# Attention's two narrow matmuls, split into halves of 64 weight columns, in a kernel of linear attention and a low-rank mixer

## The chip, the cores and the metric

The kernel runs on one core of one Trainium2 chip. The metric is the device time of one execution in microseconds. Engines are named as in the profile: PE is TensorE, and PEld is its weight loads, which run beside the matmuls; DVE is VectorE, ACT ScalarE, POOL GpSimd, SP SyncE. A line number such as L487 is a line of the kernel.

## What is computed

Eight images (`b`) with eight heads of 576 tokens and 64 features each go through linear attention, and its output through a token mixer and a two-layer network:

```python
def phi(x):                                    # 128 features, then twice 128
    proj = einsum('bhsd,df->bhsf', x, w_phi)
    proj = proj - max(abs(proj), axis=-1)
    return concatenate([exp(proj), exp(-proj)], axis=-1)
q_p, k_p = phi(q), phi(k)
kv  = einsum('bhsf,bhsd->bhfd', k_p, v)        # 256 x 64 a head
z   = sum(k_p, axis=2)
num = einsum('bhsf,bhfd->bhsd', q_p, kv)
den = einsum('bhsf,bhf->bhs', q_p, z) + 1e-06
x   = num / den                                # 576 x 512 an image
u   = x + (x.T @ U @ V).T
out = u + relu(u @ w_ch1) @ w_ch2              # 512 -> 2048 -> 512
```

## The kernel before

Heads go in pairs (class `Pair`): 32 pairs, four to an image. Of 576 tokens 512 are treated as four tiles of 128 (`NT = 4`), and the 64 left over ("tail") in matmuls of their own. `v` lies beside a column of ones, so that one matmul with 65 moving columns (`D + 1`) gives kv and z together, and another gives num and den together.

- `kv_main` (L445 to L450) makes kv of one head. For each token tile `t` and each half `f` of the 256 features, the weights are 128 features of `kp` (128 tokens by 128 columns) and the moving data is `vb`, 65 columns. The result is added up over `t` in `kv_ps`, in PSUM. That is 8 matmuls a head, behind the tail's two (`kv_tail`, L441, with both heads' 130 columns). `kv_done` then copies it out on DVE (L454).
- `out_main` (L482 to L489) makes num and den. For each of four blocks `c` of 128 tokens, two matmuls over `f` take 128 tokens of `qp` as weights and 65 columns of `kv` as moving data. That is 8 matmuls a call and two calls a pair, behind the tail's two (`out_tail`, L474). `normalize` then divides on DVE (L461 to L466).

Both work in plain float32. Such a matmul of the program appears in the profile as two weight loads and two matmuls, so 512 matmuls of the program on each of the lines L448 and L487 are 1024 records there.

The network of an image (class `Mixer`) has matmuls with 512 moving columns: `hidden` (L631) and `add` (L652), 16 blocks each. They are queued as chunks in `todo`, and `Pace` hands them out between the steps of the next image's attention, so that TensorE works on image b's network while the other engines prepare the attention of image b + 1. The last stretch of the program, from 1018 us on, holds network work alone. Before the first network is ready, matmuls on zeros (`keep_busy`, L758) are put between the steps. Within these bounds a scheduler that estimates durations sets the order of each engine's instructions.

One more matmul plays a part below: `Tokens.up` (L585) takes 128 columns of `v_all` as weights, but for the tail of every second image only 64.

Of the kernel before, what the change touches and what calls it, by code (L numbers as in the profile page):

```python
# [21 lines left out]
P = 128  # L22
# [3 lines left out]
def tile_kernel(  # L26
# [12 lines left out]
    nc = tc.nc  # L39
    B, H, S, D = q.shape  # L40
    F = w_phi.shape[1]
# [6 lines left out]
    NT = S // P  # L48
# [200 lines left out]
            nc.vector.tensor_sub(dst_lo, src, f32(dst_hi)))  # L249


    SPLIT, Q = 2, 32

    class Pair:

# [189 lines left out]
        def kv_main(self, g, kp):  # L445
            for t in range(NT):
                for f in range(2):
                    nc.tensor.matmul(  # L448
                        self.kv_v[:, f, g, :], kp[:, t, f * F:(f + 1) * F], self.vb[:, g, t, :],
                        start=False, stop=(t == NT - 1), skip_group_check=True)  # L450

        def kv_done(self):
            self.kv = small.tile([P, 2, 2, D + 1], F32, tag="kv", bufs=1, name=f"kv{self.nm}")
# [28 lines left out]
        def out_main(self, s, qp, x):  # L482
            xp = self.ps(f"xp{s}_", True)
            xv = xp[:, 0:NT * (D + 1)].rearrange("p (c e) -> p c e", e=D + 1)
            for c in range(NT):
                for f in range(2):
                    nc.tensor.matmul(  # L487
                        xv[:, c, :], qp[:, f, c * P:(c + 1) * P],
                        self.kv[:, f, c // 2 if self.split else s, :],  # L489
                        start=(f == 0), stop=(f == 1))  # L490
            if not self.split:
                h = self.h0 + s
                self.normalize(s, xv, x[:, :, h * D:(h + 1) * D])
                return
            xo = x.rearrange("p (s z) c -> p s z c", s=2)[:, s, :, self.h0 * D:(self.h0 + 2) * D]
            self.normalize(s, xv, xo.rearrange("p z (g d) -> p g z d", g=2))
# [452 lines left out]
```

## Time and profile before

| | |
|---|---|
| time, median of 2 runs | 1218.99 us (1218.80 to 1219.19) |
| the profiled execution, its own time | 1219.22 us |
| its span in the profile | 1217.4 us |
| PE busy, PEld busy | 1193.5 us (98%), 1029.9 us (85%) |
| DVE, ACT, POOL busy | 667.5, 537.2, 204.9 us (55%, 44%, 17%) |
| granted TensorE clock, mean over the span | 0.995 |

About 1.8 us of the profiled execution lie outside the span. Busy times of PE and PEld count an instruction from its issue to its modelled end, and neighbours overlap; how far apart neighbours start tells more than how long one lasts. A timeline row merges neighbours of one kind: its start, its length to the last one's end, and their number after the x.

### The profile page before, as it was taken

How to read it: one execution, taken by the hardware profiler on the slowest of the kernel's cores; microseconds unless marked ns; L12 is line 12 of the kernel's file. 1: busy time of each engine (PE TensorE's matmuls, PEld its weight loads, DVE VectorE, ACT ScalarE, POOL GpSimd, SP SyncE). 2: the span in 40 equal slices, each digit the busy share in tenths (PEclk: the TensorE clock that was granted, in tenths of full speed). 3: DMA queues.
4: the chain of work that ended last, by engine and by line, in shares of the span. 5: the costliest groups of instructions: out<-in, count | busy, mean ns of one | idle time of the engine just before them, and what ended most of it. 6: DMA issues, size and time to landing. Idle time of an engine off the chain costs nothing.

```text
span 1217.4 us, 18242 instructions
## 1 busy us (share of the span) xinstructions
PE 1193.5 (98%) x6669; PEld 1029.9 (85%) x6669; DVE 667.5 (55%) x1482; ACT 537.2 (44%) x1151; POOL 204.9 (17%) x154
## 2 busy tenths in 40 slices
PE   6999998999999999999999999999999999999998
PEld 5977887888888888888888888888888888888886
DVE  5667678765566556764647556765656542311211
ACT  5778787454443545344435454344444431111110
POOL 3334444211110111011111111011101110000000
PEclk8999999999999999999999999999999999999999
DMA  4686121331235123431244123521343015410201
GB/s 115 218 273 238 48 62 30 104 99 30 65 95 111 42 48 87 87 99 30 66 121 108 29 54 85 130 49 29 93 102 99 1 53 145 119 35 1 69 1 35
DMA packets 248290, 100.61 MB, mean 83 GB/s; under 512 B 215304, under 2 KB 227848, under 8 KB 248200
## 3 DMA queue, kind: packets, MB, share of 16 engines
q1 hardware_dynamic: 246928, 98.16, 30.9%
q10 hardware_dynamic: 1272, 1.28, 0.4%
q8 instruction: 53, 0.87, 0.3%
q14 instruction: 37, 0.30, 0.1%
HBM read 78.41 MB, written 20.97 MB: 82 GB/s over the span
## 4 chain that ended last, share of the span: by engine, by line
PE 88%; DVE 5%; DMA 2%; ACT 2%; SPq 1%; issue 1%; POOL 0%; DVEq 0%; ACTq 0%; POOLq 0%
PE ph L631 31%; PE o L652 30%; PE kv_ps L448 8%; PE xp L487 8%; PE pk L404 2%; PE pp L567 1%; PE kv_ps L441 1%; PE xpt L474 1%; PE pq L427 1%; PE pq L428 1%; SPq L270 1%; PE pq L432 1%; DVE w L240 1%; PE vp L585 1%; PE pk L389 1%
## 5 line engine op out<-in xcount | busy, mean ns | idle before, releaser
L631 PE MATMUL ph<-uT_hi,w 128*128 128x512 f32 x1152 | 389.3, 395 | 1.7 <-ACT uT_hi L248 1.1
L652 PE MATMUL o<-w,h_hi 128*128 128x512 f32 x1152 | 327.7, 395 | 0.7 <-ACT h_hi L636 0.7
L631 PEld LDWEIGHTS ph<-uT_hi,w 128*128 128x128 f32 x1152 | 216.3, 188 | 46.8 <-ACT uT_hi L248 1.8
L652 PEld LDWEIGHTS o<-w,h_hi 128*128 128x128 f32 x1152 | 211.1, 188 | 41.9 <-ACT h_hi L636 1.4
L631 PE MATMUL ph<-uT_lo,w 128*128 128x512 f32 x576 | 225.0, 391 | 0.3 <-DVE uT_lo L249 0.3
L636 ACT ACTIVATE h_hi<-ph 128x512 fp32r<-128x512 f32 x144 | 86.0, 597 | 278.9 <-PE ph L631 268.0
L637 DVE SCALAR_TENSOR_TENSOR h_lo<-ph,h_hi 128x512 fp32r<-128x512 f32 x144 | 98.7, 685 | 176.7 <-ACT h_hi L636 175.4
L652 PE MATMUL o<-w,h_lo 128*128 128x512 f32 x576 | 192.2, 395 | 0.0
L368 POOL PARTITION_ALL_REDUCE qp<-qp x64 | 127.0, 1984 | 296.8 <-ACT qp L367 274.8
L487 PEld LDWEIGHTS xp<-kv,qp 128*128 128x128 f32 x1024 | 122.6, 192 | 5.4 <-ACT w L239 0.8
L448 PEld LDWEIGHTS kv_ps<-vb,kp 128*128 128x128 f32 x1024 | 124.3, 192 | 2.8
L631 PEld LDWEIGHTS ph<-uT_lo,w 128*128 128x128 f32 x576 | 108.3, 188 | 21.6 <-DVE uT_lo L249 0.8
L487 PE MATMUL xp<-kv,qp 128*128 128x65 f32 x1024 | 122.9, 272 | 1.1 <-DVE x L466 0.7
L448 PE MATMUL kv_ps<-vb,kp 128*128 128x65 f32 x1024 | 123.7, 270 | 0.0
L652 PEld LDWEIGHTS o<-w,h_lo 128*128 128x128 f32 x576 | 105.2, 188 | 20.5 <-DVE h_lo L637 0.2
L358 ACT ACTIVATE kp<-kp 128x512 f32<-128x512 f32 x64 | 40.4, 632 | 125.9 <-DVE kp L355 88.7
L368 POOL PARTITION_ALL_REDUCE qp_t<-qp_t x32 | 27.3, 853 | 401.1 <-ACT qp_t L367 401.1
L324 DVE TENSOR_TENSOR T<-raw,T 64x512 fp32r<-64x512 f32 x96 | 68.2, 711 | 34.0 <-ACT T L323 31.5
L323 ACT CAST T<-raw 64x512 fp32r<-64x512 f32 x96 | 59.4, 618 | 34.7 <-PE pq L428 26.0
L320 DVE STREAM_TRANSPOSE raw<-raw 128x512 f32<-128x512 f32 x48 | 34.1, 711 | 67.8 <-DMA raw<-in_q_dram 24.8
L370 ACT ACTIVATE qp<-qp 128x512 f32<-128x512 f32 x64 | 40.4, 632 | 50.6 <-DVE qp L369 50.1
L145 POOL INT64_ADD w_ab<-w_ab x32 | 44.9, 1404 | 67.8 <-DVE w_ab L141 63.0
(125 smaller groups left out, 1324.2 us busy)
## 6 DMA issues: line engine op xcount, KB each, us to landing
words<-in_moe_w_ch_dram SPq DMA_DIRECT2D x32, 512.0 KB, 8.4
w<-kept SPq DMA_DIRECT2D x30, 512.0 KB, 4.0
vb<-in_v_dram SPq DMA_DIRECT2D x64, 128.0 KB, 2.4
u_dram<-x SPq DMA_DIRECT2D x32, 256.0 KB, 2.1
st<-u_dram SPq DMA_DIRECT2D x16, 512.0 KB, 3.8
out_dram<-st SPq DMA_DIRECT2D x32, 256.0 KB, 2.3
y<-u_dram SPq DMA_DIRECT2D x112, 64.0 KB, 2.2
raw<-in_k_dram SPq DMA_DIRECT2D x192, 32.0 KB, 1.8
```

What stands on the lines that cost most here:

```text
L145: nc.gpsimd.int64_add(a64, a64, b64)
L323: nc.scalar.copy(out=m[here, s, :], in_=x_[here])
L324: nc.vector.tensor_sub(m[there, s, :], x_[here], f32(m[here, s, :]))
L358: nc.scalar.activation(out=kp[:, :, 0:F], in_=kp[:, :, F:2 * F], func=AF.Exp)
L368: nc.gpsimd.partition_all_reduce(qp[:, 0, :], qp[:, 1, :], P, ReduceOp.absmax)
L370: nc.scalar.activation(out=qp[:, 0, :], in_=qp[:, 1, :], func=AF.Exp)
L448: nc.tensor.matmul(self.kv_v[:, f, g, :], kp[:, t, f * F:(f + 1) * F], self.vb[:, g, t, :], start=False, stop=(t == NT - 1), skip_group_ch ...
L487: nc.tensor.matmul(xv[:, c, :], qp[:, f, c * P:(c + 1) * P], self.kv[:, f, c // 2 if self.split else s, :], start=(f == 0), stop=(f == 1))
L631: nc.tensor.matmul(ph, w1_part(f, l, c), r[:, c, :], start=(n == 0), stop=(n == 3 * NCC - 1))
L636: on_act = nc.scalar.activation(out=h_hi, in_=ph, func=AF.Relu)
L637: on_dve = nc.vector.scalar_tensor_tensor(out=h_lo, in0=ph, scalar=0.0, in1=f32(h_hi), op0=ALU.max, op1=ALU.subtract)
L652: ins = nc.tensor.matmul(self.o[t], l[:, cs], w2_t[f][:, r, :], start=(f == 0 and n == 0), stop=(f == NFC - 1 and n == 2))
```

## The change

Each matmul of `kv_main` and of `out_main` becomes two. The first takes the first 64 of the 128 weight columns and writes partitions 0 to 63 of the same PSUM tile, the second takes the other 64 columns and writes partitions 64 to 127. The moving data is the same for both and is read twice. The built program gives these matmuls a tile of 128 rows by 64 columns, at column 0 and at column 64. The tails' matmuls (L441 and L474, which become L441 and L477) stay whole.

```diff
-    SPLIT, Q = 2, 32
+    SPLIT, Q, H = 2, 32, P // 2
...
         def kv_main(self, g, kp):
             for t in range(NT):
                 for f in range(2):
-                    nc.tensor.matmul(
-                        self.kv_v[:, f, g, :], kp[:, t, f * F:(f + 1) * F], self.vb[:, g, t, :],
-                        start=False, stop=(t == NT - 1), skip_group_check=True)
+                    for i in range(2):
+                        r_ = slice(i * H, (i + 1) * H)
+                        nc.tensor.matmul(
+                            self.kv_v[r_, f, g, :], kp[:, t, f * F + i * H:f * F + (i + 1) * H],
+                            self.vb[:, g, t, :], start=False, stop=(t == NT - 1),
+                            skip_group_check=True)
...
                 for f in range(2):
-                    nc.tensor.matmul(
-                        xv[:, c, :], qp[:, f, c * P:(c + 1) * P],
-                        self.kv[:, f, c // 2 if self.split else s, :],
-                        start=(f == 0), stop=(f == 1))
+                    for i in range(2):
+                        nc.tensor.matmul(
+                            xv[i * H:(i + 1) * H, c, :],
+                            qp[:, f, c * P + i * H:c * P + (i + 1) * H],
+                            self.kv[:, f, c // 2 if self.split else s, :],
+                            start=(f == 0), stop=(f == 1))
```

The scheduler's estimates change with it, so the order around the split matmuls moves a little. On PE, kv of pair 1 of image 2 stood like this before (`kp_1_0` and `kp_1_1` are the features of its two heads, `pq` is a projection of q, `ph` belongs to the network):

```order
L441 MATMUL kv_ps_1_2762<-vt_96,kp_1_t 128x130 x2
L448 MATMUL kv_ps_1_2762<-vb_97,kp_1_0_2588 128x65 x8
L427 MATMUL pq_2_1_2773<-T_2_1_2373,w_hl 128x512
L428 MATMUL pq_2_1_2773<-T_2_1_2373,w_hl 128x512
L448 MATMUL kv_ps_1_2762<-vb_97,kp_1_1_2640 128x65 x8
L631 MATMUL ph_2_2810<-uT_hi_2484,w_2_1074 128x512
```

and stands like this in the changed program:

```order
L441 MATMUL kv_ps_1_3050<-vt_96,kp_1_t 128x130 x2
L450 MATMUL kv_ps_1_3050<-vb_97,kp_1_0_2860 64x65 x16
L427 MATMUL pq_2_1_3069<-T_2_1_2629,w_hl 128x512
L428 MATMUL pq_2_1_3069<-T_2_1_2629,w_hl 128x512
L450 MATMUL kv_ps_1_3050<-vb_97,kp_1_1_2920 64x65 x16
L378 MATMUL pkt_2_3156<-w_hl,tail_T_2_3033 128x128
```

Eight matmuls in a row became sixteen in a row, upper and lower half in turn, and the order around them is nearly the same: the projection `pkt` has moved up.

The other place is the output of pair 2 of the same image on PE, before (`xp` is its PSUM tile, `pk` a projection of k, `o` belongs to the network):

```order
L474 MATMUL xpt_2_3190<-kv_2_3121,qp_2_t 128x130 x2
L487 MATMUL xp_2_2_3201<-kv_2_3121,qp_2_0_2996 128x65 x8
L404 MATMUL pk_2_3_3227<-w_hl,T_2_3_3048 128x256 x2
L631 MATMUL ph_7_3251<-uT_hi_2484,w_7_1556 128x512
L631 MATMUL ph_7_3251<-uT_lo_2485,w_7_1556 128x512
```

and after:

```order
L636 MATMUL ph_7_3595<-uT_lo_2757,w_7_1740 128x512
L491 MATMUL xp_2_2_3537<-kv_2_3457,qp_2_0_3316 64x65 x16
L404 MATMUL pk_2_3_3571<-w_hl,T_2_3_3368 128x256 x2
L404 MATMUL pk_2_3_3576<-w_hl,T_2_3_3368 128x256 x2
L636 MATMUL ph_7_3595<-uT_hi_2756,w_7_1740 128x512 x2
```

Here too the sixteen stand together, now between network matmuls. Over the whole program the 1024 matmuls stood in 155 unbroken stretches, and the 2048 stand in 167.

## The prediction

> **What bounds the kernel now.** I read the page's first and fourth part first, to see which engine sets the end; then the busy times by stage, to see where that holds; then single rows, to see what one of the matmuls to be split costs.
>
> ```profile
> span 1217.4 us, 18242 instructions
> PE 1193.5 (98%) x6669; PEld 1029.9 (85%) x6669; DVE 667.5 (55%) x1482; ACT 537.2 (44%) x1151; POOL 204.9 (17%) x154
> PE 88%; DVE 5%; DMA 2%; ACT 2%; SPq 1%; issue 1%; POOL 0%; DVEq 0%; ACTq 0%; POOLq 0%
> PE ph L631 31%; PE o L652 30%; PE kv_ps L448 8%; PE xp L487 8%; PE pk L404 2%; PE pp L567 1%; PE kv_ps L441 1%; PE xpt L474 1%; PE pq L427 1%; PE pq L428 1%; SPq L270 1%; PE pq L432 1%; DVE w L240 1%; PE vp L585 1%; PE pk L389 1%
> ```
>
> TensorE is busy 98% of the span and is 88% of the chain that ended last. The two lines to be split are 16% of that chain, so the change touches what sets the time. By stage (window in us, its length, then busy us and instructions of PE, PEld, DVE, ACT, POOL, the granted clock, DMA):
>
> ```profile
> 0.00:30.00 30.00, 19.81 (x108) 16.02 (x109) 14.99 (x44) 15.39 (x38) 10.25 (x25) 0.83 0.45 117
> 60.00:95.00 35.00, 32.88 (x225) 27.22 (x224) 23.69 (x58) 24.81 (x56) 14.32 (x11) 1.00 0.88 286
> 95.00:230.00 135.00, 129.38 (x740) 111.79 (x738) 99.35 (x204) 105.62 (x207) 59.67 (x42) 1.00 0.30 87
> 495.00:629.00 134.00, 134.00 (x770) 116.90 (x769) 80.54 (x182) 59.81 (x133) 18.94 (x12) 1.00 0.32 75
> 895.00:1018.00 123.00, 123.00 (x697) 107.18 (x696) 63.82 (x150) 46.00 (x101) 13.85 (x9) 1.00 0.25 66
> 1018.00:1217.40 199.40, 194.22 (x855) 159.72 (x854) 43.63 (x66) 25.08 (x43) 0.00 (x0) 1.00 0.20 54
> ```
>
> From 95 to 1018 us PE has hardly a pause (134.00 of 134 in the middle image), at the full clock. DVE, next in line, is busy 80.54 of these 134 us. Until 95 us the matmuls on zeros fill PE's pauses, so time saved on PE there is mostly not time saved. After 1018 us no split matmul stands.
>
> What does one of them cost? First long stretches of weight loads, then two groups of the page:
>
> ```profile
> 155.25 3.65 PEld L448 LDWEIGHTS kv_ps<-vb,kp 128*128 128x128 f32 x32
> 508.56 1.53 PEld L487 LDWEIGHTS xp<-kv,qp 128*128 128x128 f32 x13
> 503.56 0.61 PE L474 MATMUL xpt<-kv,qp_t 128*128 128x130 f32 x4
> L487 PEld LDWEIGHTS xp<-kv,qp 128*128 128x128 f32 x1024 | 122.6, 192 | 5.4 <-ACT w L239 0.8
> L448 PEld LDWEIGHTS kv_ps<-vb,kp 128*128 128x128 f32 x1024 | 124.3, 192 | 2.8
> L474 PE MATMUL xpt<-kv,qp_t 128*128 128x130 f32 x128 | 19.5, 274 | 0.0
> ```
>
> The last of 32 loads starts 3.65 - 0.19 = 3.46 us after the first, which is 31 steps of **112 ns**; the row of 13 gives 1.34 / 12 = 112 again. A matmul with twice the moving columns (L474, 130) steps no slower: one lasts 0.27, so (0.61 - 0.27) / 3 = 113 ns. With 65 columns the moving data would therefore need only about 56 ns, and in the split lines the **weight load** of 128 columns sets the pace, with the array streaming half the time. The two groups hold 2048 loads, so they take 2048 x 112 = 229 us of PE.
>
> **The change part by part.** Each program matmul is two records (two loads, two matmuls), 224 ns. Split, it becomes four of each: two for the upper half, then two for the lower. Loads and matmuls on these lines go from 2048 to 4096.
>
> A load of 64 columns: the nearest rows are those of L585, the one line that has both widths.
>
> ```profile
> L585 PEld LDWEIGHTS vp<-pst,v_all 128*128 128x128 f32 x36 | 6.7, 189 | 1.2
> L585 PEld LDWEIGHTS vp<-pst,v_all 128*64 128x64 f32 x4 | 0.5, 135 | 0.1
> L758 PEld LDWEIGHTS <-zeros 128*128 128x128 bf16 x37 | 4.3, 120 | 4.7 <-issue 3.3 <-DVE zeros L753 1.2
> ```
>
> Half the columns last 54 ns less (189 - 135), about half of the 112 ns step: a load of 64 costs some 56 ns, and a matmul of 65 moving columns some 56 ns whatever its weight columns. Four of each, strictly one behind the other on one path, are 4 x 56 = 224 ns: exactly what is paid now. So halving alone brings nothing, and **everything hangs on whether the two halves work beside each other**. No row of before shows two 64-column tiles at once. The bounds per program matmul: fully side by side, the upper half's two loads take 112 ns and the lower half's run a step behind; nothing overlapping at all, every half record costs a load and then a matmul, 4 x (56 + 56) = 448 ns. Between these, the third row above speaks for the fast end: 128 bf16 columns load in 120 ns where 128 float32 columns take 189, so the array takes in columns faster than the 112 ns step. I take the fast end with the delay that the order causes: matmuls start in order, and the records stand upper, upper, lower, lower. The lower half's first load can start as soon as the upper's second has, its own second 56 ns later, and the next upper one a few ns behind that: about 2 x 56 = 112, and I put **120 ns**. That saves 104 ns a program matmul.
>
> How many of them count:
>
> ```profile
> 60.00:95.00 35.00, 6.13 (x48) 5.83 (x48) 1.00 0.88 286
> 95.00:230.00 135.00, 15.41 (x128) 15.28 (x128) 1.00 0.30 87
> 895.00:1018.00 123.00, 15.15 (x128) 15.07 (x128) 1.00 0.25 66
> ...
> 95.00:230.00 135.00, 15.37 (x128) 15.46 (x128) 1.00 0.30 87
> 895.00:1018.00 123.00, 11.37 (x96) 11.42 (x96) 1.00 0.25 66
> ```
>
> The first three rows are L487 alone, the last two L448. From 95 us on there are seven stretches of an image each: 7 x 128 = 896 records of L487, and 6 x 128 + 96 = 864 of L448, whose first 32 of an image come one stretch sooner. 1760 records are 880 program matmuls: 880 x 104 ns = **91.5 us**. The other 144 stand before 95 us, where matmuls on zeros and waits take up what is saved; I count nothing for them (at most 144 x 104 = 15 us, if that stage were bound by PE).
>
> Changing between 128 and 64 columns: four such changes exist, behind L585. Here is one (the second L585 matmul has 64 columns):
>
> ```profile
> 362.62 0.39 PE L652 MATMUL o<-w,h_lo 128*128 128x512 f32 x1
> 362.85 0.62 PE L585 MATMUL vp<-pst,v_all 128*128 128x512 f32 x2
> 363.08 0.42 PEld L652 LDWEIGHTS o<-w,h_hi 128*128 128x128 f32 x2
> 363.31 0.62 PE L652 MATMUL o<-w,h_hi 128*128 128x512 f32 x2
> ```
>
> From the first L585 matmul to the L652 behind it are 0.46 us for two, where a step at one width is 0.23 (362.62 to 362.85): the change costs about 10 ns at most. The changed order has 167 stretches of split matmuls, hence 334 changes: 334 x 10 ns = 3.3 us. A stretch also fills and drains its two halves once, about one half's 28 to 56 ns not overlapped, 167 x 0.03 = 5 us. Together **+8 us**.
>
> The Trainium skill's page "TensorEngine Tiling (Array Packing)", section Key Properties, says that changing the tiling mode drains the engine. A full drain by the rows here would be what a matmul lasts beyond its step, 0.39 - 0.23 = 0.16 us, or 334 x 0.16 = 53 us in place of 3.3; the row above shows 0.01, so I do not take it, but it is a rival below.
>
> The rest I cost at nothing. The moved instructions on ACT, DVE and the queues are covered by PE's work: at 134.00 busy of 134, nothing they do is waited for. Were that cover gone, the late one would be DVE; with PE's image at 134 - 13 = 121 us it still has 40 us of slack. kv's copy (L454) and the division (L461) wait for the last matmul of a stretch, which comes sooner.
>
> The sum against the profiled execution's own 1219.22 us (span 1217.4, 1.8 outside): 1219.2 - 91.5 + 8 = **1136 us**. The median of the runs, 1218.99, is the same within 0.3 us.
>
> **The rivals.** *One path for loads.* If loads of the two halves queue behind each other, four at 56 ns are the same 224 ns, however freely the matmuls run. The loads' steps in before never fall clearly under 108 to 112 ns, which fits a single path. With the changes of width and 0 to 7 ns of overhead a program matmul (the 112 ns step is some 5 above twice the 54 of the L585 rows) that is 0 to +6 us, and +3 to +8: 1222 to 1233, about **1225**. Decisive point: the step of four loads stays at or above 216 ns.
>
> *Strict order.* The halves overlap, but a load starts only when the matmul ahead of it has started. How long after its load's start a matmul is issued, two neighbouring rows show:
>
> ```profile
> 364.01 0.19 PEld L379 LDWEIGHTS pkt<-w_hl,tail_T 128*128 128x128 f32 x1
> 364.06 0.28 PE L379 MATMUL pkt<-w_hl,tail_T 128*128 128x128 f32 x1
> ```
>
> It is 0.05 us, half of a load's step; for 64 columns then 28 ns. A half's second matmul comes 56 ns behind its first, and the other half's first 28 behind that: 2 x (56 + 28) = 168 ns, 56 saved: 880 x 56 = 49, less 8, **1178**.
>
> *A drain at each change of width.* As forecast, with 53 us in place of 3.3: 1136 + 50 = **1186**. The L585 rows speak against it; but there 512 moving columns may hide what 65 do not.
>
> *Slower: a pair keeps its price whatever its width.* If a load cannot run under a matmul on the same rows, or issuing sets the step, each load and matmul go on taking 112 ns, and a split matmul costs 448 in place of 224. Place: all of L450 and L491. Price: 880 x 224 = 197 us, and up to 32 more before 95 us, so 1219 + 197 + 8 = **1424**. It decides slower by 2% from (224 + 28) / 4 = 63 ns a pair. For it: 65 and 130 moving columns step alike at 112, and no stretch of before steps faster. Against it: the load at 363.08 starts at the very start of the 64-column matmul (362.85 + 0.23), so it does run under one.
> On this the Trainium skill's page "TensorE: Matmul & The Clock Gate", Part 3, "The mechanism", says that weight loads overlap matmuls in flight only where the row group differs; the halves share all rows, so by it this rival would hold. The row at 363.08 shows such a load under a matmul on all 128 rows; no run here shows it between two 64-column tiles.
>
> **How the numbers follow.** Forecast 0.40, strict order 0.08, drain 0.07, one path 0.30, slower 0.15. The first three are faster by over 2% (24 us, about what a measurement of this kernel can tell from no change): 0.55 faster, 0.30 within 2%, 0.15 slower. The forecast's own range is 1110 to 1165: all 1024 matmuls counting takes off 15 more, a step of 140 in place of 120 adds 18. As faster and unchanged hold most of the chance, the range goes from **1110 to 1233**, and leaves out the slower rival and little else.
>
> **What would show it.** In the changed profile: the loads on L450 and L491 step at about 30 ns on average (forecast), 42 (strict order), 56 (one path) or 112 (slower). In the forecast the first lower matmul starts while the second upper one still streams, and an image takes about 121 us in place of 134. A gap of over 0.1 us at the first network matmul behind a stretch would show the drain. The network's steps (0.23 us) should not move. The forecast is wrong if loads of the two halves never overlap, or if the image stays at 134 us although they do; then DVE's chain has taken over.

## The result, and the profile after

The changed kernel takes **1175.44 us** (median of two runs, 1175.22 to 1175.66) against 1218.99: 0.964 times the time before, 95% interval 0.960 to 0.968. Measured again on another chip it took 1178.96 (0.966, 0.965 to 0.967). So 41 to 44 us went, where the forecast was 83. From the page of the changed kernel: its span, its busy times, the chain that ended last by engine, and the two split lines:

```profile
span 1173.4 us, 22343 instructions
PE 1146.9 (98%) x8717; PEld 933.6 (80%) x8717; DVE 677.2 (58%) x1482; ACT 536.0 (46%) x1151; POOL 203.2 (17%) x154
PE 77%; DVE 7%; DMA 5%; SPq 5%; ACT 5%; issue 1%; POOL 0%; DVEq 0%; ACTq 0%; POOLq 0%
L450 PEld LDWEIGHTS kv_ps<-vb,kp 128*64 128x64 f32 x2048 | 69.4, 137 | 22.3 <-issue 13.5
L491 PEld LDWEIGHTS xp<-kv,qp 128*64 128x64 f32 x2048 | 65.8, 137 | 21.4 <-issue 8.7
```

There are twice as many weight loads on the two lines, and PEld is busy with them for 135 us in place of 247. PE is still busy 98% of the span, and what its busy time leaves of the span went only from 23.9 to 26.5 us, so it still sets the time. Its cover over the other engines is thinner: it is 77% of the chain that ended last, where it was 88%. New are the 22.3 and 21.4 us that PEld stood idle just before these loads, about half of it put down to "issue": nothing that the profile shows was waited for. Before, the same groups had 2.8 and 5.4.

One image in the middle, in the windows of both traces (after, then before; columns as in the prediction's stages):

```profile
485.80:614.00 128.20, 127.19 (x1024) 104.14 (x1023) 81.04 (x181) 59.42 (x133) 18.98 (x12) 1.00 0.34 79
```

```profile
508.60:641.90 133.30, 133.30 (x766) 116.26 (x765) 79.65 (x181) 59.35 (x133) 18.94 (x12) 1.00 0.32 76
```

An image takes 5.1 us less. One stretch of the outputs' matmuls shows both the gain and what eats it. The timeline of before on PE, with the matmul in front of the stretch and the one behind it:

```profile
508.33 0.39 PE L631 MATMUL ph<-uT_hi,w 128*128 128x512 f32 x1
508.56 1.89 PE L487 MATMUL xp<-kv,qp 128*128 128x65 f32 x16
510.26 0.72 PE L652 MATMUL o<-w,h_lo 128*128 128x512 f32 x2
```

and of after, the same kind of place, with the loads:

```profile
515.16 0.40 PE L636 MATMUL ph<-uT_hi,w 128*128 128x512 f32 x1
515.49 1.15 PE L491 MATMUL xp<-kv,qp 128*64 128x65 f32 x32
515.49 1.01 PEld L491 LDWEIGHTS xp<-kv,qp 128*64 128x64 f32 x32 [0.36 <-DVE den_t L465]
516.57 0.50 PE L636 MATMUL ph<-uT_hi,w 128*128 128x512 f32 x1
516.91 0.40 PE L636 MATMUL ph<-uT_lo,w 128*128 128x512 f32 x1
```

From the stretch's first matmul to the one behind it: 510.26 - 508.56 = 1.70 us for 16 records before, 516.57 - 515.49 = 1.08 us for 32 after. The loads' row gives the step: the last of 32 starts 1.01 - 0.14 = 0.87 us after the first, **28 ns** on average. In the trace the records stand in twos, 6 ns apart, and the next two follow 52 ns later: 58 ns for two, 117 for a program matmul. The two halves do work beside each other.

But look at the start. A 512-column matmul steps by 0.23 us, and the first split one comes 515.49 - 515.16 = **0.33 us** behind the network's; before it was 508.56 - 508.33 = 0.23. Its load starts only there, 0.07 us before the matmul ahead ends (515.16 + 0.40 = 515.56); in the kernel before, such a load started within a few ns of the start of the matmul ahead. At the end the next network load waits in the same way, until 516.57, 0.15 us behind the stretch's last matmul (at 516.42) and again 0.07 us before that one ends (515.49 + 1.15 = 516.64). The network's matmul there is followed 516.91 - 516.57 = 0.34 us later, much as in the kernel before (0.33).

The row puts the loads' 0.36 us of waiting down to `den_t` on DVE, but DVE does not set this start. In the trace 164 of the 167 stretches begin with a load 71 to 73 ns before the modelled end of the matmul ahead, whoever the profile names, and 164 of the loads behind a stretch start so too; of the 155 stretches before, none does.

What a stretch costs beyond its own work follows from the network's matmul in front to the second one behind it. After: 516.91 - 515.16 = 1.75 us, less two network steps (0.46) and 32 records at 58 ns for two (0.93), leaves **0.36 us**. Before: the second L652 starts at 510.26 + 0.72 - 0.39 = 510.59, so 2.26 us, less 0.46, are 1.80 for 16 x 0.112 = 1.79: nothing is left over. The expectations below go by a rounder 0.3 us.

### The profile page after: what moved, and what is told of

Same layout as the page of the kernel before. It is cut to its first block, busy times and chain, and to the rows that moved or that the text cites. A ratio compares the mean times of both kernels' runs of the same rounds, so it can differ in the third digit from the quotient of the medians.

```text
span 1173.4 us, 22343 instructions
## 1 busy us (share of the span) xinstructions
PE 1146.9 (98%) x8717; PEld 933.6 (80%) x8717; DVE 677.2 (58%) x1482; ACT 536.0 (46%) x1151; POOL 203.2 (17%) x154
## 4 chain that ended last, share of the span: by engine, by line
PE 77%; DVE 7%; DMA 5%; SPq 5%; ACT 5%; issue 1%; POOL 0%; DVEq 0%; ACTq 0%; POOLq 0%
PE ph L636 28%; PE o L657 27%; PE kv_ps L450 5%; PE xp L491 5%; SPq L622 3%; PE pk L404 2%; DMA raw<-in_q_dram 2%; PE pq L427 2%; PE pp L572 2%; SPq L270 1%; PE kv_ps L441 1%; DVE x L591 1%; DMA y<-u_dram 1%; PE xpt L477 1%; PE pq L428 1%
## 5 line engine op out<-in xcount | busy, mean ns | idle before, releaser
L657 PE MATMUL o<-w,h_hi 128*128 128x512 f32 x1152 | 321.6, 395 | 3.0 <-ACT h_hi L641 2.8
L657 PE MATMUL o<-w,h_lo 128*128 128x512 f32 x576 | 188.4, 395 | 0.8 <-DVE h_lo L642 0.7
L657 PEld LDWEIGHTS o<-w,h_lo 128*128 128x128 f32 x576 | 105.8, 188 | 23.5 <-DVE h_lo L642 2.4
L450 PEld LDWEIGHTS kv_ps<-vb,kp 128*64 128x64 f32 x2048 | 69.4, 137 | 22.3 <-issue 13.5
L491 PEld LDWEIGHTS xp<-kv,qp 128*64 128x64 f32 x2048 | 65.8, 137 | 21.4 <-issue 8.7
L450 PE MATMUL kv_ps<-vb,kp 128*64 128x65 f32 x2048 | 82.4, 226 | 0.1
L491 PE MATMUL xp<-kv,qp 128*64 128x65 f32 x2048 | 76.1, 225 | 0.8 <-ACT qp L370 0.4
```

The source lines that it names most:

```text
L450: nc.tensor.matmul(self.kv_v[r_, f, g, :], kp[:, t, f * F + i * H:f * F + (i + 1) * H], self.vb[:, g, t, :], start=False, stop=(t == NT - ...
L491: nc.tensor.matmul(xv[i * H:(i + 1) * H, c, :], qp[:, f, c * P + i * H:c * P + (i + 1) * H], self.kv[:, f, c // 2 if self.split else s, :] ...
L657: ins = nc.tensor.matmul(self.o[t], l[:, cs], w2_t[f][:, r, :], start=(f == 0 and n == 0), stop=(f == NFC - 1 and n == 2))
```

## Experiments

Theory A is what these rows suggest: the halves run side by side, and each stretch pays some 0.3 us for changing the width and changing back. Theory B: the change of width costs nothing, and the missing gain went into waits for DVE and ACT. Times in brackets are ratios to the kernel before, run beside it on the same chip, with 95% intervals.

**One line at a time.** `kv_only` splits kv alone, `out_only` the outputs alone; the other function stays as in the kernel before.

> Only kv's matmuls are split; the outputs' matmuls stay 128 columns wide. Theory A (the halves run side by side, 117 ns a program matmul in place of 223, and each stretch of split matmuls pays about 0.3 us for its two changes of width): 512 x 0.106 = 54 us less 92 stretches x 0.3 = 28 leaves 26 us, of which the first image hides an eighth: about 1196 us. Theory B (changes of width cost nothing, and the missing gain of the full change was lost in waits for DVE and ACT): with half the matmuls split these engines are not yet late, so nearly all of the 54 us less an eighth shows: about 1172 us.

> Only the outputs' matmuls are split, kv's stay whole. Theory A: 512 x 0.106 = 54 us less 76 stretches x 0.3 = 23 leaves 31, less an eighth: about 1192 us. Theory B: about 1172 us, as for kv alone.

Measured: 1201.41 us (0.985, 0.983 to 0.986) and 1196.52 us (0.981, 0.980 to 0.983) beside 1220.18 before. They gain 18.8 and 23.7 us. Theory B expected some 48 from either; theory A's 24 and 28 are 4 to 5 us too high. With 0.36 us a stretch in place of 0.3 the same sums give 18.5 and 23.5. The gains add up to 42.5, the whole change's. A loss in waits that only comes when both are split would not add up so; a price that each stretch pays does.

**Both halves on one column tile.** This tells whether halving alone does something. The edit, against `kv_main` of the changed kernel (the outputs stay whole):

```diff
-                            self.kv_v[r_, f, g, :], kp[:, t, f * F + i * H:f * F + (i + 1) * H],
+                            self.kv_v[0:H, f, g, :], kp[:, t, f * F + i * H:f * F + (i + 1) * H],
```

> kv's matmuls alone are split, but both halves are sent to the upper column tile (partitions 0 to 63), so that they can't run beside each other; what belongs into the lower partitions of kv is left out. Theory A: records step at 56 ns one behind the other, 224 ns a program matmul, so the split gains nothing and 89 stretches pay 0.3 us each, less an eighth: about 1242 us. Theory A' (the change of price comes from addressing a second column tile, not from the width, as the 64-column matmul at L585 showed no price): 1219 us, no gap at a stretch's ends. Theory C (halving alone makes loads faster, wherever the halves go): faster than 1219.

Measured: 1258.16 us (1.031, 1.030 to 1.033), 38 us slower than before. A stretch of it in the timeline, with the matmuls around it:

```profile
502.94 0.39 PE L441 MATMUL kv_ps<-vt,kp_t 128*128 128x130 f32 x2
503.26 2.08 PE L449 MATMUL kv_ps<-vb,kp 128*64 128x65 f32 x32
503.26 1.94 PEld L449 LDWEIGHTS kv_ps<-vb,kp 128*64 128x64 f32 x32
505.27 0.50 PE L427 MATMUL pq<-T,w_hl 128*128 128x512 f32 x1
```

The loads step at (1.94 - 0.14) / 31 = 58 ns, one behind the other: 232 ns a program matmul, more than the 224 of the whole one. So halving by itself gains nothing, and the whole gain of the change is that the second half has a column tile of its own. The price of a stretch is there all the same, at column 0: the stretch lasts 505.27 - 503.26 = 2.01 us where 32 x 0.058 = 1.87 are work, and it starts 0.32 us behind the first of two 130-column matmuls that step at 0.11, so 0.1 late. That refutes theory A'. Theory A had expected 1242; 512 x 8 ns = 4 us more come from the step, and 89 stretches at 0.36 us instead of 0.3 add 5 us, less an eighth. Some 7 us of the slowdown I cannot place.

**More changes of width.** `kv_alt` splits kv alone, and only for token tiles 0 and 2; again against the changed kernel's `kv_main`.

```diff
-                    for i in range(2):
-                        r_ = slice(i * H, (i + 1) * H)
+                    for i in range(2 if t % 2 == 0 else 1):
+                        w = H if t % 2 == 0 else P
+                        r_ = slice(i * H, i * H + w)
                         nc.tensor.matmul(
-                            self.kv_v[r_, f, g, :], kp[:, t, f * F + i * H:f * F + (i + 1) * H],
+                            self.kv_v[r_, f, g, :], kp[:, t, f * F + i * H:f * F + i * H + w],
```

> kv's matmuls alone are split, and only for token tiles 0 and 2; tiles 1 and 3 stay whole, so that widths change in the middle of a head. Theory A: 256 program matmuls gain 0.106 us each, 27 us, and 138 stretches pay 0.3 us, 41 us; the balance of +14 less an eighth gives about 1231 us, slower than without any split. Theory B: 27 less an eighth faster, about 1195 us.

Measured: 1241.41 us (1.018, 1.016 to 1.019): 21 us slower than with no split at all, though half of kv's matmuls run side by side. Theory B falls with that. If 256 x 0.106 x 7/8 = 24 us are gained, the stretches cost 45 us; 7/8 of 138 at that are 0.37 us each.

**Fewer stretches.** kv of a pair's first head moves into the step of its second (`merge_`), and in a second form the second output moves into the step of the first as well (`merge2_`). Both were run without split matmuls too, since the order itself may cost.

```diff
         def s_kv0_q1(self):
-            self.kv_tail()
-            self.kv_main(0, self.kp0)
             self.qp1 = self.project_q(1)
 
         def s_kv1(self):
+            self.kv_tail()
+            self.kv_main(0, self.kp0)
             self.kv_main(1, self.kp1)
```

```diff
             self.out_main(0, self.qp0, x)
+            self.out_main(1, self.qp1, x)
 
         def s_out1(self, x):
-            self.out_main(1, self.qp1, x)
+            pass
```

> The kernel before with one change of order: kv of a pair's first head is made in the step of the second (with the tail's), not a step earlier. No matmul is split. All theories: the regrouping alone does little, 1215 to 1225 us. It is the yardstick for the next run; what it moves by itself is taken off there.

> The changed kernel with that same change of order: 117 stretches of split matmuls in place of 167, the same 2048 matmuls. Theory A (a stretch pays about 0.3 us for its two changes of width): 50 x 0.3 = 15 us less an eighth for the first image: about 1162 us. Theory B (the missing gain went into waits): the same as the changed kernel, 1175 us, or slower, since kv comes a step later.

> As the run before, and a pair's second output is made in the step of the first: 103 stretches. Theory A: 64 stretches less than the changed kernel, 64 x 0.3 x 7/8 = 17 us: about 1158 us. Theory B: 1175 us or more.

> The changed kernel once more, as the yardstick for the two runs beside it: 1175 us, 0.964 of before.

> The changed kernel with both regroupings, 103 stretches in place of 167. Theory A with the cost of regrouping (13 us in the kernel without split matmuls): 1170 to 1172 us, 3 to 5 us under the changed kernel; by the rival that the first measurement was luck of the chip, the same as the changed kernel.

> The kernel before with both regroupings and no split matmul. Theory A: the split is worth 44 us at 167 stretches and was worth 54 at 117, that is 0.2 us a stretch, so at 103 it is worth 57 and this kernel takes about 1228 us. If the price of a stretch were nothing, the split would be worth 44 here too: about 1215 us.

| order | stretches of split matmuls | whole, us | split, us | the split's gain |
|---|---|---|---|---|
| as it was | 167 | 1220.32 | 1178.96 | 41.4 |
| `merge_` | 117 | 1232.60 | 1178.94 | 53.7 |
| `merge2_` | 103 | 1230.11 | 1172.90 | 57.2 |

The first and third row were run together, the second in another run. The regrouping itself cost 10 to 13 us, where I had expected none, and so `merge_after` was not faster than the changed kernel as theory A had said. But the split's gain grows with every stretch that goes: 57.2 - 41.4 = 15.8 us for 64 stretches, 0.25 us each. The first `merge2_after` took 1170.91 (0.960, 0.959 to 0.962), where theory A had expected 1158. Run beside the changed kernel it took 1172.90 (0.961, 0.960 to 0.962) against 1178.96 (0.966, 0.965 to 0.967): it beats both kernels, the changed one by half a per cent.

A double stretch shows that the price belongs to the stretch and not to its matmuls. In `merge2_after`:

```profile
519.91 0.39 PE L637 MATMUL ph<-uT_hi,w 128*128 128x512 f32 x1
520.22 2.09 PE L491 MATMUL xp<-kv,qp 128*64 128x65 f32 x64
522.24 0.50 PE L637 MATMUL ph<-uT_hi,w 128*128 128x512 f32 x1
522.58 0.39 PE L637 MATMUL ph<-uT_lo,w 128*128 128x512 f32 x1
```

From 519.91 to 522.58 are 2.67 us; less two network steps (0.46) and 64 records at 58 ns for two (1.86), 0.35 is left, as for 32 records. That the runs give only 0.25 goes with waits that the regrouped order brings. PE of `merge2_after_again` waited for the activation of the network's next block on ACT:

```profile
PE o L658 <- ACT h_hi L642: 14.6, 16, 1.8
```

In the changed kernel this was 2.8 us, and in `merge2_before` 2.8. What PE's busy time leaves of the span is 1170.8 - 1130.3 = 40.5 us in `merge2_after_again`, against 26.5 in the changed kernel: 14 us more, about what theory A's 1158 missed by. By busy times alone the split is worth 1199.5 - 1130.3 = 69.2 us in the `merge2_` order and 1193.5 - 1146.9 = 46.6 in the old one: 22.6 us for 64 stretches, 0.35 each. In `merge_before` the same wait is part of the 13 us that its order costs:

```profile
PE o L652 <- ACT h_hi L636: 8.4, 8, 1.8
```

In the kernel before this was 0.7 us. The 10 us of `merge2_before` are not explained by it.

**The tails as well.** `merge2_tails` is `merge2_after` with the tails' 130-column matmuls split like the others (`kv_tail`, `out_tail`).

> As the run before, and the tails' 128 matmuls with 130 moving columns are split as well; 118 stretches. Their step of 112 ns a record is set by load and matmul alike, so side by side two halves should give 117 ns a program matmul in place of 224. Theory A: 128 x 0.107 = 13.7 us less 15 more stretches x 0.3 = 4.5, less an eighth: some 8 us under the run before, about 1150 us. Rival (the moving data of the two halves share one path, so that 130 columns twice take as long as before): no gain, and 4 us more for the stretches, about 1162 us.

Measured: 1174.28 us (0.962, 0.961 to 0.964), 3.4 us over `merge2_after` beside it, with intervals that overlap: no gain in any case. My own figure there was wrong. Its timeline at a tail in front of kv:

```profile
511.45 0.66 PE L258 MATMUL kv_ps<-vt,kp_t 128*64 128x130 f32 x8
511.84 0.37 PEld L457 LDWEIGHTS kv_ps<-vb,kp 128*64 128x64 f32 x8
511.95 0.34 PE L457 MATMUL kv_ps<-vb,kp 128*64 128x65 f32 x6
```

Eight records take 511.95 - 511.45 = 0.50 us; four whole ones took 4 x 0.112 = 0.45. In the trace two halves start 6 ns apart and the next two 110 ns later: the halves do stream side by side, so the rival's reason (a shared path) is not it. But 130 columns need some 110 ns to stream whether the weights have 64 columns or 128, and that was already the whole matmul's step. So splitting helped here only where the load, not the moving data, set the step, and the 15 stretches more, at 0.36 us, are 5 us of price.

## Why the prediction was right in direction and half in size

*What bounds the kernel, and what a split matmul costs.* Right. PE stayed the bound, the weight load of 128 columns was what 65 moving columns waited for, and halving alone brings nothing (58 ns a half on one tile, forecast 56).

*The halves side by side.* Right, nearly to the number: 117 ns a program matmul, forecast 120. The order I had assumed, upper, upper, lower, lower, is not what the trace shows; the records come in twos, 6 ns apart.

*The first image.* I had counted nothing there, of at most 15 us. In the traces the second image's first output matmul starts at 92.0 us in place of 96.8, so that stage did give 4.8 us.

*The change of width.* This step failed: "334 x 10 ns = 3.3 us", with 5 us more for filling and draining. Each stretch pays 0.36 us, and 167 x 0.36 = 60 us, where I had 8. With it, and 117 ns in place of 120, the sum gives 1219 - 94 + 60 x 7/8 = 1178; the first image's 4.8 us and 2.6 us more of idle time on PE bring it to about 1175. Measured were 1175 to 1179. The 10 ns came from L585's 64-column matmuls. They still step by 236 ns in the changed kernel, between 128-column ones, so the row was read rightly; it was no measure for this case. What sets it apart is not the column position, since `kv_same` pays at column 0. It differs in number type (its operands are float32r, the split ones float32) and in moving columns (512 against 65); which of the two decides was not tried.

*The rival of a drain at each change.* It put 53 us in place of 3.3 and came out at 1186, for a chance of 0.07; I set it aside for the L585 row. Its mechanism is the one that the runs show: at both ends of a stretch the next load is held back until 0.07 us before the matmul ahead ends. The sign written down for it, a gap of over 0.1 us at the first network matmul behind a stretch, is there with 0.15. The Trainium skill's rule in "TensorEngine Tiling (Array Packing)", Key Properties, agrees with these rows, though not with L585's 236 ns, whose tile is 128*64 too. The rival's price per change, 0.16 us, is near half of the 0.36 for two. *Strict order*, 1178, fits the total but not the rows: loads step at 28 ns, not 42. A total that agrees does not show the mechanism. *One path* is refuted by the 28 ns too, and *slower* as well: in `kv_same` each load runs under the matmul before it on the same rows (58 ns a pair, where a load and a matmul in turn would need 112). So what the Trainium skill's page "TensorE: Matmul & The Clock Gate", Part 3, "The mechanism", says of row groups does not hold between two 64-column matmuls here.

*The range.* The forecast's own range, 1110 to 1165, does not hold the 1175. The wide one, to 1233, does, but only since it had to take in the rival of one path, which is not what happened: that much was luck.

*Nothing else waits.* Nearly right. In the changed kernel PE's loads waited 4.6 us for `h_hi` on ACT and 3.3 for `h_lo` on DVE, and PE's idle time over the whole span grew by 2.6 us.

## What to carry to other kernels

Where the moving data took less time than the weight load (65 columns), splitting a float32 matmul into two column tiles let both halves load and stream at once, and it halved the step (224 to 117 ns); where the moving data already filled the load's time (130 columns) it brought nothing. Going from 128-column tiles into these 64-column ones and back held up TensorE's next load each time, 0.36 us for the two, so count the stretches, not only the matmuls: a stretch of eight program matmuls gained about 0.85 us and paid 0.36, and one of two program matmuls (`kv_alt`) paid more than it gained. A neighbour's row that seems to price a new operation has to share its number type and shape as well, or both ends of the range must be kept for it in the likeliest sum.

## What was not expected of the hardware

Two 64-column weight loads on different column tiles start 6 ns apart and both fit in 58 ns, where one 128-column load takes 112: here weight columns entered the array at two places at once. Going into 64-column tiles, the first load comes late (the matmul starts 0.33 us in place of 0.23 behind a 512-column matmul, 0.20 in place of 0.11 behind a 130-column one), and coming out the next load starts 0.15 us behind the last matmul. At both ends that is the same point, 0.07 us before the modelled end of the matmul ahead, whether that has 65, 130 or 512 moving columns. A 64-column float32 load does run under a 64-column matmul on the same rows and the same column tile (`kv_same`, 58 ns for the pair).
